# Narrowing 64-bit weights with one pass fewer, in a planned attention and MoE kernel

## The chip, the cores and the metric

One core of a Trainium2 chip runs the whole program. The metric is device time in microseconds. Three runs of the kernel before took 604.0, 604.93 and 605.22 us, a median of 604.93 us. The profiled execution took 603.86 us, of which 602.1 us lie between its first and its last instruction.

## The reference

Attention, then two gated layers, all in float32, for 4 batches of 8 heads, 512 local and 32 global positions and head size 64. The layers' weights arrive as 64-bit floats.

```python
# attention: 32 global queries see all keys; a local query sees the globals and |i-j| <= 32
out_g = sm(q_g k_all^T / 8) @ v_all
out_l = sm([q_l k_g^T / 8, where(|i-j| <= 32, q_l k_l^T / 8, -1e9)]) @ v_all
x = concat(out_g, out_l)              # (4, 544, 512) after the heads are joined

# MoE1
h = max(x @ w_in, 0)                  # 512 -> 1024
gate = sigmoid(conv over the sequence, width 3, of h)
x = (h * gate) @ w_out                # 1024 -> 512

# MoE2, with x_prev = x shifted by one position
k = max((mu_k*x + (1-mu_k)*x_prev) @ w_k, 0)
r = sigmoid((mu_r*x + (1-mu_r)*x_prev) @ w_r)
out = r * (k*k @ w_v)
```

## The kernel before

Every large product is made of three float32r matmuls: an operand is split into a rounded "hi" part and a remainder "lo", and hi*hi, hi*lo and lo*hi are added in PSUM. So each weight exists in SBUF as two tiles.

Four batches pass through attention and MoE1. Attention has a unit for each pair of heads (four units a batch): scores (`s`), masking with the row minimum on VectorE (L484), exponential on ScalarE (L491), transposes on TensorE (L500) that are copied to `eT` (L503), the product with v (L510), the division (L520 to L522), a transpose (L541) and the split into hi and lo (L548, L551). Every second unit is followed by the global queries (`glob`, L573). MoE1 of a batch (`dense`, L838) has eight blocks of H (L856, x times w_in). Each block is followed by relu (L880), three convolution taps (L889 to L898), sigmoid (L904), the product with h (L907) and the split into `gh` and `gl` (L914, L919). Then come four blocks of O (L957, times w_out), whose results are copied to a tile `xo` (L975) and stored to a DRAM tensor `x2d` (L982). There is one `xo` buffer (`XO_BUFS = 1`): the memset of its first column on GpSimd (L974) and the copies wait until the store before has landed. MoE2 (`moe2`, L1005) runs over six chunks of up to 384 tokens: K (L1094, with w_k), R (L1160, with w_r) and V (L1197, with w_v), in this order.

A 64-bit weight is narrowed to float32 (`narrow_tasks`, L701) in steps: a DMA of the raw words (SyncE's queue); the high word without its sign (L712 on ScalarE or L714 on VectorE); a maximum with the smallest normal value (`fmax`, L717, on VectorE or GpSimd); a shift left by 3 with a mask (L721, VectorE); the sign (and top bits) put back and then the low word's top bits put in (L727, two instructions, VectorE). After it come hi (L792) and lo (L795). w_in and w_out are narrowed at the start in pieces of 128x512, conv_w in one small piece. w_k, w_r and w_v are narrowed early, during the MoE1 of the batches 0 to 2, in 40 pieces of 128x256 (16, 8 and 16), which are stored to DRAM as float32 (L757). Later they are loaded again (L780) and only split: w_k and w_r when attention is done, w_v when the last H has let go of w_in's tiles, whose place it takes.

The order of instructions on each engine is written by a planner in the file (`Plan.schedule`, L198). It keeps a clock for each engine, for TensorE's speed and for each ring of buffers, takes among the tasks that could start earliest the one with the smallest key, and picks for a task with alternatives the engine that would end it first, with a bias for each engine and phase (`DVE_BIAS` and the others). The keys come from `STEP0`, `SLOT`, `LEAD`, `GAP` and the lags. VectorE and GpSimd slow each other in the plan by a factor (`PORT`, `shared`, `POOL_SLOW`). The plan only fixes the order; on the chip every instruction waits for semaphores.

Of the kernel before, what the change touches and what calls it, by code (L numbers as in the profile page):

```python
# [34 lines left out]
EST = 256  # L35
F64_MIN = float(np.array(0x38000000, np.uint32).view(np.float32))

# [4 lines left out]
ET_BUFS = 3  # L42
W2_BUFS = 6
E_STEP = 16
XB = 6
T_START = 10000
STEP0 = 6737
T_DENSE = 38000
SLOT = 72484
LEAD = 14181  # L50
GAP = 2397
GAP1 = 1480
STEPS_H = 6
E_BUFS = 4
H_FRAC = 0.5
LAG_TE = 5000
LAG_PV = 10538
LAG_G = 7061
LEAD_Q = 4000
# [4 lines left out]
LAG_TX = 9367  # L64
WINDOW = 43
FILL_MIN = 553
FILL_MARGIN = 276
FILL_START = 6
FILL_RATE = 0.478
PENALTY = 166  # L70
PHASES = (60e3, 105e3, 320e3, 375e3)
DVE_BIAS = (1550, 807, 684, 1523, 580)
ACT_BIAS = (411, 657, 466, 1004, 80)
POOL_BIAS = (6, 0, 235, 0, 113)
H_BUFS = 5
C_BUFS = 3
G_BUFS = 4
XO_BUFS = 1
V_BUFS = 3
# [3 lines left out]
QT_BUFS = 3  # L83
KT_BUFS = 4

# [61 lines left out]
class Plan:  # L147
# [16 lines left out]
    @staticmethod  # L164
    def latency(a, b):
        if a == "-" or b == "-":
            return 0
        if a == "DMA":
# [29 lines left out]
    def schedule(self):  # L198
# [13 lines left out]
        free["PE"] = 1130.0  # L212
        dve_port = False
        while cand:
            ests = []
            for t in cand:
                e = 0.0
                need = {}
                for b in t.take:
                    for r in b.rings:  # L220
                        need[r] = need.get(r, 0) + 1
                if any(len(slots[r]) < n for r, n in need.items()):
                    continue
                for r, n in need.items():
                    e = max(e, sorted(slots[r])[n - 1])
# [55 lines left out]
            if t.eng != "-":  # L281
                free[t.eng] = t.end
            if t.eng == "DVE":
                dve_port = PORT.get(t.kind, 1.0) > 1.0
            for b in t.bufs:
                owed[b] -= 1
                ends[b] = max(ends.get(b, 0.0), t.end + (1900 if t.eng == "DMA" else 200))
# [25 lines left out]
def shared(cost, left, slow):

    if left <= 0:
        return cost
    return cost * slow if left >= cost * slow else left + cost - left / slow

# [19 lines left out]
def attn_moe_kernel(  # L338
# [362 lines left out]
    def narrow_tasks(nm, load, n, braw, bmag, after, early):  # L701
# [36 lines left out]
        c = add("DVE", 68 + 534 * f, lambda: for_(1, -0x40000000, ALU.bitwise_and), deps=[c],  # L738
                use=[bmag, braw], name=f"sgn{nm}")
# [21 lines left out]

    def split_weights(nm, src, nt, ncol, pool, tag, rings, after=(), early=None):
        w = {}
# [7 lines left out]
        for k in range(nt):  # L771
            for c in range(0, ncol, WST):
                bm = buf(rings[1])
                if early:
                    t, sts = early[k, c]
                    state = {}

                    def load(t=t, c=c, bm=bm, state=state, k=k):
                        state["mag"] = alloc(bm, [P, WST], F32, f"{nm}{k}_{c}")
                        nc.sync.dma_start(out=state["mag"], in_=t[:, c : c + WST])  # L780

                    d = add("DMA", 730, load, deps=sts + [al], take=[bm], name=f"ld{nm}{k}_{c}")
                else:
                    def load(raw, k=k, c=c):
                        nc.sync.dma_start(
                            out=raw, in_=words(src[P * k : P * (k + 1), c : c + WST], "p (n t) -> p n t")
                        )

                    d, state = narrow_tasks(f"{nm}{k}_{c}", load, WST, buf(rings[0]), bm, [al], None)

                def fhi(copy, k=k, c=c, state=state):
                    copy(w["hi"][:, k, c : c + WST], state["mag"])  # L792

                def flo(e, k=k, c=c, state=state):
                    e.tensor_sub(w["lo"][:, k, c : c + WST], state["mag"], w["hi"][:, k, c : c + WST].bitcast(F32))  # L795

                h = add("ACT", 520, lambda fhi=fhi: fhi(nc.scalar.copy), deps=[d], use=[bm], name=f"hi{nm}{k}_{c}",
                        alts=[("DVE", 335, lambda fhi=fhi: fhi(nc.vector.tensor_copy))])
                l = add("POOL", 1225, lambda flo=flo: flo(nc.gpsimd), deps=[h], use=[bm], name=f"lo{nm}{k}_{c}",
                        alts=[("DVE", 602, lambda flo=flo: flo(nc.vector))])  # L800
                done[k, c] = [h, l]
        return w, done
# [35 lines left out]
    def dense(b):  # L838
# [403 lines left out]
    for b in range(B):  # L1242
# [3 lines left out]
        if b == B - 2:  # L1246
            turn_e = [0]

            def after():
# [84 lines left out]
```

## Time and profile before

| | |
|---|---|
| median of three runs | 604.93 us |
| profiled execution | 603.86 us, span 602.1 us |
| busy TensorE, VectorE, ScalarE, GpSimd | 565.3, 395.7, 285.5, 228.2 us |
| mean granted TensorE clock | 0.949 |
| DMA | 67.80 MB, nearly all through one queue |

A busy time is the union of an engine's instructions, so overlapping matmuls count once. PEclk is the granted clock as a share of the full one. In a group of instructions, the idle time "before" an instruction is what its engine stood still, and behind the arrow stands what ended it. A line number is that of the kernel before.

### The profile page before, as it was taken

How to read it: one execution, taken by the hardware profiler on the slowest of the kernel's cores; microseconds unless marked ns; L12 is line 12 of the kernel's file. 1: busy time of each engine (PE TensorE's matmuls, PEld its weight loads, DVE VectorE, ACT ScalarE, POOL GpSimd, SP SyncE). 2: the span in 40 equal slices, each digit the busy share in tenths (PEclk: the TensorE clock that was granted, in tenths of full speed). 3: DMA queues.
4: the chain of work that ended last, by engine and by line, in shares of the span. 5: the costliest groups of instructions: out<-in, count | busy, mean ns of one | idle time of the engine just before them, and what ended most of it. 6: DMA issues, size and time to landing. Idle time of an engine off the chain costs nothing. (4 is left out here: it accounts for less than half of the span.)

```text
span 602.1 us, 14503 instructions
## 1 busy us (share of the span) xinstructions
PE 565.3 (94%) x5790; PEld 515.3 (86%) x5790; DVE 395.7 (66%) x969; ACT 285.5 (47%) x632; POOL 228.2 (38%) x320
## 2 busy tenths in 40 slices
PE   8697957997999979999999899999999999999998
PEld 6585946996989879889899799889889899898897
DVE  3689999847699954999958976441826637434211
ACT  4585856614588623677466634504305225134040
POOL 3647767622243302333111554937602203203150
PEclk8787986797999979999999989999999999999999
DMA  8957701567515675005480432020110200100000
GB/s 310 339 195 246 275 10 52 179 180 233 179 54 197 193 255 174 20 3 167 170 255 16 137 126 64 8 81 18 39 67 1 62 35 1 53 19 1 36 19 35
DMA packets 34627, 67.80 MB, mean 113 GB/s; under 512 B 5120, under 2 KB 14592, under 8 KB 34560
## 3 DMA queue, kind: packets, MB, share of 16 engines
q1 hardware_dynamic: 34560, 66.88, 33.4%
q8 instruction: 45, 0.74, 0.5%
q14 instruction: 22, 0.18, 0.1%
HBM read 52.71 MB, written 14.16 MB: 111 GB/s over the span
## 5 line engine op out<-in xcount | busy, mean ns | idle before, releaser
L856 PE MATMUL ph<-x,win_hi 128*128 128x256 f32 (+1 forms) x512 | 102.4, 298 | 0.0
L957 PE MATMUL po<-gl,wout_hi 128*128 128x256 f32 (+1 forms) x256 | 77.8, 304 | 7.1 <-POOL gl L919 5.2
L957 PE MATMUL po<-gh,wout_hi 128*128 128x256 f32 (+1 forms) x256 | 79.9, 312 | 2.8 <-ACT gh L914 2.8
L856 PEld LDWEIGHTS ph<-x,win_hi 128*128 128x128 f32 x512 | 81.2, 192 | 1.4
L957 PE MATMUL po<-gh,wout_lo 128*128 128x256 f32 (+1 forms) x256 | 76.9, 300 | 0.0
L856 PE MATMUL ph<-x,win_lo 128*128 128x256 f32 (+1 forms) x256 | 74.2, 290 | 0.0
L1112 ACT ACTIVATE robuf<-pk 128x384 f32<-128x384 f32 (+1 forms) x48 | 22.7, 472 | 91.8 <-PE pk L1094 91.4
L898 DVE SCALAR_TENSOR_TENSOR c<-h,convw,c 128x544 f32<-128x544 f32 x64 | 60.2, 959 | 4.6 <-POOL h L877 2.3
L1094 PE MATMUL pk<-xkh,wkk_lo 128*128 128x384 f32 (+1 forms) x192 | 62.7, 327 | 0.0
L1094 PE MATMUL pk<-xkh,wkk_hi 128*128 128x384 f32 (+1 forms) x192 | 62.7, 327 | 0.0
L1094 PE MATMUL pk<-xkl,wkk_hi 128*128 128x384 f32 (+1 forms) x192 | 62.7, 327 | 0.0
L957 PEld LDWEIGHTS po<-gl,wout_hi 128*128 128x128 f32 x256 | 51.7, 202 | 8.0 <-POOL gl L919 5.9
L957 PEld LDWEIGHTS po<-gh,wout_hi 128*128 128x128 f32 x256 | 51.7, 202 | 4.5 <-ACT gh L914 3.2
L1197 PE MATMUL pv<-wvv_lo,k2h 128*128 128x512 f32 (+1 forms) x144 | 54.4, 378 | 0.0
L1197 PE MATMUL pv<-wvv_hi,k2h 128*128 128x512 f32 (+1 forms) x144 | 54.4, 378 | 0.0
L1197 PE MATMUL pv<-wvv_hi,k2l 128*128 128x512 f32 (+1 forms) x144 | 54.4, 377 | 0.0
L1210 DVE TENSOR_TENSOR robuf<-pv,robuf 128x512 f32<-128x512 f32 (+1 forms) x18 | 11.9, 661 | 63.5 <-PE pv L1197 63.4
L957 PEld LDWEIGHTS po<-gh,wout_lo 128*128 128x128 f32 x256 | 51.7, 202 | 0.0
L856 PEld LDWEIGHTS ph<-x,win_lo 128*128 128x128 f32 x256 | 49.0, 192 | 0.0
L491 ACT ACTIVATE e<-e 128x128 f32<-128x128 f32 x128 | 39.8, 392 | 8.8 <-DVE e L484 8.7
L1160 PE MATMUL pr<-wrr_hi,xrbuf 128*128 128x512 f32 x136 | 43.7, 395 | 0.0
L1094 PEld LDWEIGHTS pk<-xkl,wkk_hi 128*128 128x128 f32 x192 | 36.1, 188 | 0.2
(224 smaller groups left out, 1294.9 us busy)
## 6 DMA issues: line engine op xcount, KB each, us to landing
v<-in_v_l_dram SPq DMA_DIRECT2D x16, 910.0 KB, 7.1
x2d<-xo SPq DMA_DIRECT2D x16, 272.5 KB, 2.9
qT<-in_q_l_dram SPq DMA_DIRECT2D x16, 256.0 KB, 3.6
kT<-in_k_l_dram SPq DMA_DIRECT2D x16, 256.0 KB, 4.7
wout_0r<-in_moe_w_out_dram SPq DMA_DIRECT2D x8, 512.0 KB, 4.5
out_dram<-robuf SPq DMA_DIRECT2D x16, 256.0 KB, 2.0
win_0r<-in_moe_w_in_dram SPq DMA_DIRECT2D x4, 512.0 KB, 8.0
win_512r<-in_moe_w_in_dram SPq DMA_DIRECT2D x4, 512.0 KB, 7.3
```

What stands on the lines that cost most here:

```text
L491: nc.scalar.activation(be.tile[:, P * i : P * (i + 1)], be.tile[:, P * i : P * (i + 1)], AF.Exp, bias=be.tile[:, SL + i : SL + i + 1], sca ...
L856: nc.tensor.matmul(pm, lhsT=w[:, k, P * m : P * (m + 1)], rhs=x[:, s0:s1], start=(k == 0 and n == 0), stop=(k == KT - 1 and n == 2),)
L898: e.scalar_tensor_tensor(bc.tile, bh.tile[:, k : k + S], convw[:, FT * k + m : FT * k + m + 1], bc.tile, op0=ALU.mult, op1=ALU.add,)
L957: nc.tensor.matmul(pm, lhsT=w[:, k, P * m : P * (m + 1)], rhs=g[:, k % 2, s0:s1], start=(k == 0 and n == 0), stop=(k == FT - 1 and n == 2),)
L1094: nc.tensor.matmul(bp.tile[:, :n], lhsT=w[:, k, P * m : P * (m + 1)], rhs=x[:, :n], start=(k == 0 and i == 0), stop=(k == KT - 1 and i == 2),)
L1112: e.activation(kk()[:, :n], bp.tile[:, :n], AF.Relu)
L1160: nc.tensor.matmul(bp.tile, lhsT=x[:, P * j : P * (j + 1)], rhs=w[:, k], start=(k == 0 and i == 0), stop=(k == KT - 1 and i == 2),)
L1197: nc.tensor.matmul(bp.tile, lhsT=x, rhs=w[:, k, c0:c1], start=(k == 0 and i == 0), stop=(k == FT - 1 and i == 2),)
L1210: nc.vector.tensor_mul(o()[:, c0:c1], bp.tile, r()[:, c0:c1])
```

## The change

- Narrowing: the sign-free high word and the maximum are replaced by one multiplication of the high word, read as a float32, by 2^-112 on ScalarE, with no alternative on VectorE. The shift no longer masks, and the instruction that puts the sign back takes one bit.
- `w_v` is not narrowed early any more. `split_weights` narrows it from the raw words in 16 pieces of 128x256 (`EST`), with three raw buffers and three result buffers in the pool that opens after attention; as before, this can begin when the last H is done. `W2_BUFS` goes from 6 to 3.
- MoE1's output has two `xo` buffers, and its store is issued from ScalarE's queue; the planner knows that queue as an engine "AQ".
- In the planner, VectorE and GpSimd no longer slow each other by a factor. An instruction that uses the port waits until the port is free, and holds it for its whole time (VectorE kinds in `PORT`) or for 0.9 or 0.5 of it (GpSimd).
- Keys, biases, the planner's window and some ring sizes have other values (`KT_BUFS` 4 to 3).

```diff
-F64_MIN = float(np.array(0x38000000, np.uint32).view(np.float32))
+REBIAS = 2.0**-112
-W2_BUFS = 6
+W2_BUFS = 3
+W2R_BUFS = 3
-STEP0 = 6737
+STEP0 = 7159
-SLOT = 72484
-LEAD = 14181
-GAP = 2397
-GAP1 = 1480
+SLOT = 67764
+LEAD = 3854
+GAP = -8076
+GAP1 = 5974
-WINDOW = 43
+WINDOW = 25
-DVE_BIAS = (1550, 807, 684, 1523, 580)
-ACT_BIAS = (411, 657, 466, 1004, 80)
-POOL_BIAS = (6, 0, 235, 0, 113)
+DVE_BIAS = (1550, 1239, 579, 1173, -209)
+ACT_BIAS = (299, 685, -307, 215, 80)
+POOL_BIAS = (-54, 564, 227, -666, -3480)
-XO_BUFS = 1
+XO_BUFS = 2
-KT_BUFS = 4
+KT_BUFS = 3
...
-                    if o[0] == "DVE":
-                        c = shared(c, free.get("POOL", 0.0) - x, PORT.get(t.kind, 1.0))
-                    elif o[0] == "POOL":
-                        c = shared(c, free.get("DVE", 0.0) - x if dve_port else 0.0, POOL_SLOW)
+                    if holds_port(o[0], t.kind):
+                        x = max(x, free.get("PORT", 0.0))
...
+            if h := holds_port(t.eng, t.kind):
+                free["PORT"] = max(free.get("PORT", 0.0), t.start + h * t.cost)
...
+def holds_port(eng, kind):
+
+    if eng == "POOL":
+        return 0.0 if kind == "on" else 0.5 if kind in ("cv", "gn") else 0.9
+    return 1.0 if eng == "DVE" and kind in PORT else 0.0
...
-        def fabs(e):
+        def fmag():
             state["mag"] = alloc(bmag, [P, max(n, EST)], F32, f"{nm}m")[:, :n]
-            hw = state["raw"][:, :n, 1]
-            if e is nc.scalar:
-                e.activation(state["mag"], hw.bitcast(F32), AF.Abs)
-            else:
-                e.tensor_scalar(state["mag"].bitcast(I32), hw, 0x7FFFFFFF, None, op0=ALU.bitwise_and)
-
-        def fmax(e):
-            e.tensor_scalar(state["mag"], state["mag"], F64_MIN, None, op0=ALU.max)
+            nc.scalar.activation(state["mag"], state["raw"][:, :n, 1].bitcast(F32), AF.Copy, scale=REBIAS)
...
-            nc.vector.tensor_scalar(
-                bits, bits, 3, 0x3FFFFFF8, op0=ALU.logical_shift_left, op1=ALU.bitwise_and
-            )
+            nc.vector.tensor_scalar(bits, bits, 3, None, op0=ALU.logical_shift_left)
...
-        c = add("DVE", 60 + 275 * f, lambda: fmax(nc.vector), deps=[c], use=[bmag], name=f"max{nm}",
-                alts=[("POOL", 70 + 1386 * f, lambda: fmax(nc.gpsimd))])
...
-                "DMA", 900, lambda bo=bo, m=m: nc.sync.dma_start(out=x2d[b][m], in_=bo.tile),
+                "AQ", 900, lambda bo=bo, m=m: nc.scalar.dma_start(out=x2d[b][m], in_=bo.tile),
...
-                     for nm, src, nt, ncol in (("wkk", w_k, KT, FF), ("wrr", w_r, KT, DM), ("wvv", w_v, FT, DM))}
+                     for nm, src, nt, ncol in (("wkk", w_k, KT, FF), ("wrr", w_r, KT, DM))}
...
-    wvv, wvv_done = split_weights("wvv", w_v, FT, DM, lambda: winp, "wa", (None, "w2mag"), h_done + [att_done], early["wvv"])
+    wvv, wvv_done = split_weights("wvv", w_v, FT, DM, lambda: winp, "wa", ("w2raw", "w2mag"), h_done + [att_done], st=EST)
```

## Rows read from the trace of the kernel before

**Rows 1.** The page's busy times: busy us, share of the span, instructions.

```profile
PE 565.3 (94%) x5790; PEld 515.3 (86%) x5790; DVE 395.7 (66%) x969; ACT 285.5 (47%) x632; POOL 228.2 (38%) x320
```

**Rows 2.** Chain that ended last: start, length, engine, tile, line, instructions.

```profile
363.94 16.65 PE pk L1094 x96
...
388.98 16.35 PE pv L1197 x72
405.33 16.64 PE pk L1094 x96
```

**Rows 3.** Busy times by stretch, which may overlap; then clock, DMA share, GB/s.

```profile
0.00:45.00 45.00, 37.24 (x819) 31.17 (x819) 27.85 (x130) 26.63 (x73) 21.63 (x37) 0.85 0.78 282
45.00:110.00 65.00, 51.33 (x599) 45.80 (x589) 64.33 (x112) 39.99 (x84) 49.25 (x54) 0.78 0.41 140
60.00:90.00 30.00, 23.05 (x198) 22.23 (x198) 29.83 (x42) 19.68 (x41) 22.32 (x29) 0.90 0.42 146
75.00:120.00 45.00, 34.78 (x474) 31.42 (x473) 41.92 (x86) 26.06 (x57) 32.07 (x31) 0.73 0.23 79
140.00:150.00 10.00, 9.20 (x171) 8.34 (x172) 9.38 (x34) 5.72 (x15) 2.93 (x3) 0.71 0.70 221
150.00:335.00 185.00, 179.34 (x2510) 168.27 (x2509) 150.84 (x446) 117.01 (x253) 51.09 (x112) 0.98 0.43 139
335.00:389.00 54.00, 51.04 (x322) 48.80 (x321) 37.65 (x46) 25.54 (x53) 33.44 (x33) 0.97 0.28 85
```

**Rows 4.** Groups on VectorE, 60 to 90 us: count, busy us, mean ns, idle before.

```profile
L727 DVE SCALAR_TENSOR_TENSOR wout_0m<-wout_0r,wout_0m 128x512 int32<-128x512 int32 x14 | 15.0, 1081 | 0.0
L898 DVE SCALAR_TENSOR_TENSOR c<-h,convw,c 128x544 f32<-128x544 f32 x6 | 6.9, 1178 | 0.0
L721 DVE TENSOR_SCALAR wout_0m<-wout_0m 128x512 int32<-128x512 int32 x8 | 4.3, 563 | 0.0
L717 DVE TENSOR_SCALAR wout_0m<-wout_0m 128x512 f32<-128x512 f32 x4 | 4.0, 1008 | 0.0
```

**Rows 5.** Lines 727, 898, 721, 717, whole run: min/median/max ns, first and last start.

```profile
L727 DVE SCALAR_TENSOR_TENSOR wout_0m<-wout_0r,wout_0m x16: 673/750/1819, 60.1 to 94.0; 128x512 int32<-128x512 int32 x16
...
L898 DVE SCALAR_TENSOR_TENSOR c<-h,convw,c x64: 765/778/1859, 65.5 to 339.8; 128x544 f32<-128x544 f32 x64
...
L721 DVE TENSOR_SCALAR wout_0m<-wout_0m x8: 412/415/1395, 59.5 to 89.6; 128x512 int32<-128x512 int32 x8
...
L717 POOL TENSOR_SCALAR wout_0m<-wout_0m x4: 1503/1838/1908, 56.8 to 71.2; 128x512 f32<-128x512 f32 x4
L717 DVE TENSOR_SCALAR wout_0m<-wout_0m x4: 414/1001/1618, 62.5 to 86.3; 128x512 f32<-128x512 f32 x4
```

**Rows 6.** Timeline of VectorE and GpSimd, 337 to 340 us: start, length.

```profile
337.33 0.78 DVE L898 SCALAR_TENSOR_TENSOR c<-h,convw,c 128x544 f32<-128x544 f32 x1
337.56 1.74 POOL L919 TENSOR_TENSOR gl<-c,gh 128x544 fp32r<-128x544 f32 x1 [4.88 <-DVE gh L914]
338.02 1.86 DVE L907 TENSOR_TENSOR c<-c,h 128x544 f32<-128x544 f32 x1
```

**Rows 7.** Timeline, 139 to 141 us: start, length, engine; idle before, releaser.

```profile
139.58 0.68 ACT L975 COPY xo<-po 128x256 f32<-128x256 f32 x2 [2.98 <-DMA x2d<-xo]
...
140.14 1.10 ACT L503 COPY eT<-pe 128x512 f32<-128x512 f32 x2
...
140.80 0.45 PE L510 MATMUL o<-v,eT 128*32 128x65 f32 x8 [3.67 <-ACT eT L503]
```

**Rows 8.** Waits by pair: us in total, times, longest.

```profile
ACT xo L975 <- DMA x2d<-xo: 14.7, 7, 4.5
```

**Rows 9.** Lines 727 and 721 on w_v's first half pieces, min/median/max ns.

```profile
L727 DVE SCALAR_TENSOR_TENSOR ewvv_0m<-ewvv_0r,ewvv_0m x16: 406/418/640, 221.0 to 298.5; 128x256 int32<-128x256 int32 x16
...
L721 DVE TENSOR_SCALAR ewvv_0m<-ewvv_0m x8: 279/282/433, 220.7 to 297.5; 128x256 int32<-128x256 int32 x8
```

**Rows 10.** DMA issues: KB each, median us to landing.

```profile
ewvv_256r<-in_moe_w_v_dram SPq DMA_DIRECT2D x8, 256.0 KB, 4.0
```

More of the change, by code (lines that the diff above doesn't have):

```diff
@@ L46 @@
 T_START = 10000
-STEP0 = 6737
+STEP0 = 7159
 T_DENSE = 38000
-SLOT = 72484
-LEAD = 14181
-GAP = 2397
-GAP1 = 1480
+SLOT = 67764
+LEAD = 3854
+GAP = -8076
+GAP1 = 5974
 STEPS_H = 6
 E_BUFS = 4
[L55 to L58, printed above, removed]
+H_FRAC = 0.498
+LAG_TE = 3810
+LAG_PV = 10382
+LAG_G = 5305
 LEAD_Q = 4000
@@ L69 @@
 FILL_RATE = 0.478
-PENALTY = 166
+PENALTY = 394
 PHASES = (60e3, 105e3, 320e3, 375e3)
-DVE_BIAS = (1550, 807, 684, 1523, 580)
-ACT_BIAS = (411, 657, 466, 1004, 80)
-POOL_BIAS = (6, 0, 235, 0, 113)
+DVE_BIAS = (1550, 1239, 579, 1173, -209)
+ACT_BIAS = (299, 685, -307, 215, 80)
+POOL_BIAS = (-54, 564, 227, -666, -3480)
 H_BUFS = 5
@@ L167, in latency @@
             return 0
-        if a == "DMA":
+        if a in ("DMA", "AQ"):
             return 1900
@@ L212, in schedule @@
         free["PE"] = 1130.0
-        dve_port = False
         while cand:
@@ L282, in schedule @@
                 free[t.eng] = t.end
-            if t.eng == "DVE":
-                dve_port = PORT.get(t.kind, 1.0) > 1.0
+            if h := holds_port(t.eng, t.kind):
+                free["PORT"] = max(free.get("PORT", 0.0), t.start + h * t.cost)
             for b in t.bufs:
                 owed[b] -= 1
-                ends[b] = max(ends.get(b, 0.0), t.end + (1900 if t.eng == "DMA" else 200))
+                ends[b] = max(ends.get(b, 0.0), t.end + (1900 if t.eng in ("DMA", "AQ") else 200))
                 if not owed[b]:
@@ L304 @@
 WEIGHTS = ("win", "wout", "wkk", "wrr", "wvv", "conv")
-POOL_SLOW = 1.17
 PORT = {
-    "cv": 1.55, "mu": 1.65, "gl": 1.65, "gh": 3.0, "max": 1.6, "shl": 1.6, "sgn": 1.15, "low": 1.15, "lo": 1.65,
-    "hi": 3.0, "d": 1.65, "xxk": 1.9, "xxr": 1.9, "xkh": 3.0, "xrh": 3.0, "xkl": 1.65, "xrl": 1.65, "sq": 1.65,
-    "k2h": 3.0, "k2l": 1.65, "gn": 2.0,
-}
[L313 to L317, printed above, removed]
+    "cv", "mu", "gl", "gh", "max", "shl", "sgn", "low", "lo", "hi", "d", "xxk", "xxr", "xkh", "xrh", "xkl", "xrl", "sq",
+    "k2h", "k2l", "gn",
+}
+def holds_port(eng, kind):
+    if eng == "POOL":
+        return 0.0 if kind == "on" else 0.5 if kind in ("cv", "gn") else 0.9
+    return 1.0 if eng == "DVE" and kind in PORT else 0.0
 def bias(eng, x):
@@ L351, in attn_moe_kernel @@
         "x0": XB, "x1": XB, "h": H_BUFS, "c": C_BUFS, "gh": G_BUFS, "gl": G_BUFS, "xo": XO_BUFS,
-        "w2mag": W2_BUFS,
+        "w2mag": W2_BUFS, "w2raw": W2R_BUFS,
     })
@@ L732, in narrow_tasks @@
         a = add("DMA", 1460 * f, fload, deps=after, take=[braw], name=f"ld{nm}")
-        c = add("ACT", 40 + 480 * f, lambda: fabs(nc.scalar), deps=[a], take=[bmag], use=[braw], name=f"abs{nm}",
-                alts=[("DVE", 60 + 275 * f, lambda: fabs(nc.vector))])
-        c = add("DVE", 60 + 275 * f, lambda: fmax(nc.vector), deps=[c], use=[bmag], name=f"max{nm}",
-                alts=[("POOL", 70 + 1386 * f, lambda: fmax(nc.gpsimd))])
+        c = add("ACT", 90 + 490 * f, fmag, deps=[a], take=[bmag], use=[braw], name=f"abs{nm}")
         c = add("DVE", 60 + 275 * f, fshift, deps=[c], use=[bmag], name=f"shl{nm}")
-        c = add("DVE", 68 + 534 * f, lambda: for_(1, -0x40000000, ALU.bitwise_and), deps=[c],
+        c = add("DVE", 68 + 534 * f, lambda: for_(1, -0x80000000, ALU.bitwise_and), deps=[c],
                 use=[bmag, braw], name=f"sgn{nm}")
@@ L760, in early_narrow, with split_weights @@
         return pieces
-    def split_weights(nm, src, nt, ncol, pool, tag, rings, after=(), early=None):
+    def split_weights(nm, src, nt, ncol, pool, tag, rings, after=(), early=None, st=WST):
         w = {}
@@ L771, in split_weights @@
         for k in range(nt):
-            for c in range(0, ncol, WST):
+            for c in range(0, ncol, st):
                 bm = buf(rings[1])
@@ L785, in load @@
                         nc.sync.dma_start(
-                            out=raw, in_=words(src[P * k : P * (k + 1), c : c + WST], "p (n t) -> p n t")
+                            out=raw, in_=words(src[P * k : P * (k + 1), c : c + st], "p (n t) -> p n t")
                         )
-                    d, state = narrow_tasks(f"{nm}{k}_{c}", load, WST, buf(rings[0]), bm, [al], None)
+                    d, state = narrow_tasks(f"{nm}{k}_{c}", load, st, buf(rings[0]), bm, [al], None)
                 def fhi(copy, k=k, c=c, state=state):
-                    copy(w["hi"][:, k, c : c + WST], state["mag"])
+                    copy(w["hi"][:, k, c : c + st], state["mag"])
                 def flo(e, k=k, c=c, state=state):
[L795 to L801, printed above, removed]
+                    e.tensor_sub(w["lo"][:, k, c : c + st], state["mag"], w["hi"][:, k, c : c + st].bitcast(F32))
+                f = st / WST
+                h = add("ACT", 40 + 480 * f, lambda fhi=fhi: fhi(nc.scalar.copy), deps=[d], use=[bm], name=f"hi{nm}{k}_{c}",
+                        alts=[("DVE", 60 + 275 * f, lambda fhi=fhi: fhi(nc.vector.tensor_copy))])
+                l = add("POOL", 70 + 1155 * f, lambda flo=flo: flo(nc.gpsimd), deps=[h], use=[bm], name=f"lo{nm}{k}_{c}",
+                        alts=[("DVE", 68 + 534 * f, lambda flo=flo: flo(nc.vector))])
+                done.setdefault((k, c // WST * WST), []).extend([h, l])
         return w, done
@@ L1261, in open_w2 @@
                 w2["p"] = ctx.enter_context(tc.tile_pool(name="w2", bufs=1, side="right"))
-                pools["w2mag"] = w2["p"]
+                pools["w2mag"] = pools["w2raw"] = w2["p"]
             att_done = add("-", 0, open_w2, deps=att_tasks, name="open_w2")
```

## The prediction

> **What bounds the kernel now.** I read the busy times first, then the chain that ended last, then the busy times by stretch. TensorE is busy 565.3 of 602.1 us [rows 1]. From 363.94 us on the chain is TensorE alone, K, R and V chunk after chunk without a gap: 16.65 us of K, then R, and V from 388.98 us [rows 2]. That is 238 us of the span that no other engine can shorten, as long as its operands are there. The reader should therefore look for the time ahead of 364 us, in two forms: TensorE idle, and TensorE at a low clock.
>
> The stretches show where [rows 3]. In them a clock of 1 is TensorE's upper level of 2.4 GHz and 0.5 its lower one of 1.2 GHz; a mean between is a stretch that had both. From 150 to 335 us TensorE is busy 179.3 of 185 us at a clock of 0.98, so little is left there. From 45 to 110 us it is VectorE that is full, 64.33 of 65 us, while TensorE has 51.33 us at a clock of 0.78. That is the stage in which w_out is narrowed beside the first batch's MoE1. Between 140 and 150 us the clock is 0.71 again. The price of the early stage is paid in VectorE time, and the later dips are single waits.
>
> **VectorE and GpSimd share something, and the stage pays for it.** A GpSimd instruction of 1.74 us starts at 337.56 us. A VectorE product with both inputs in SBUF, issued at 338.02 us, takes 1.86 us and ends just after it [rows 6], and the shortest times of such forms are far below: 673 ns for L727 and 765 ns for L898, with 1819 and 1859 ns at the other end [rows 5]. For 60 to 90 us I add up what VectorE lost to this, mean less shortest, by count [rows 4, 5]: L727 14 x (1081 - 673) = 5.7 us, L898 6 x (1178 - 765) = 2.5, L721 8 x (563 - 412) = 1.2, L717 4 x (1008 - 414) = 2.4, together 11.8 us. GpSimd was busy 22.32 us in it [rows 3]. So by this estimate a microsecond of GpSimd costs VectorE about 11.8 / 22.32 = 0.53 us there.
>
> **The change part by part**, against the profiled execution's 603.86 us, which lies 1.07 us under the median.
>
> *The maximum goes.* For w_out four of the eight maxima were on VectorE, 4.0 us in all [rows 4]. The other four were on GpSimd, at a median of 1838 ns [rows 5], 7.4 us, which at 0.53 gives VectorE 3.9 us back. VectorE has no gap in this stage, so I take all of it as an earlier end: 7.9 us. The upper end is that GpSimd blocks VectorE for its whole length, 4.0 + 7.4 = 11.4 us. The lower end is 0, if another engine then holds TensorE in that stage. The maxima of w_in lie mostly before 45 us, where VectorE has 27.85 of 45 us [rows 3], and I give them nothing. What is late next is the chain of ScalarE passes and GpSimd's lo parts.
>
> The Trainium skill ("SBUF — State Buffer", section "Who interferes with whom") says that the port pair of VectorE and GpSimd is locked for a whole instruction and the loser waits, not shares. The stretched product above agrees with it; the 0.53 does not contradict it, since GpSimd is not always in VectorE's way. By the rule alone the term would be the 11.4 us of the upper end, and the sum 3.5 us lower.
>
> *The first pass has ScalarE alone.* Its multiplication takes the place of the pass without a sign, and the few such passes that VectorE did go to ScalarE too. ScalarE has 25 of 65 us free in the full stage [rows 3], so I put this at nothing. If that cover were gone, a pass over a piece would cost about as much as one of the two `eT` copies of the same 512 columns that took 1.10 us together [rows 7], and for two passes it would be 1.1 us.
>
> *Two buffers for the output, stored from ScalarE's queue.* With one buffer ScalarE waited 14.7 us for landed stores, at most 4.5 us at a time [rows 8]. Most of that stands beside full matmuls. One wait does not: at 139.58 us ScalarE comes out of a wait of 2.98 us, only then copies `eT`, and TensorE has stood 3.67 us for it [rows 7]. Behind it TensorE works at 0.71 from 140 to 150 us [rows 3], which costs (1 - 0.71) x 10 = 2.9 us. With a second buffer the copy needs the store before last, so I take both back, 6.6 us. The lower end is 0 (the copy could be late for another reason), and on the wrong side stands up to 4.5 us, the longest wait of ScalarE [rows 8]: the store now stands in ScalarE's own order and waits for both copies, one of which may be VectorE's, and sigmoid, relu and the `eT` copies queue behind it. SyncE's queue loses these waits, so loads behind them start earlier; I price that at nothing, since those loads are for buffers that are needed later.
>
> *w_v narrowed late.* Its 16 pieces leave the stretch from 150 to 335 us, where VectorE had 34 us free and TensorE was full, so nothing is won there. They land between the last H, at about 335 us, and the first V at 388.98 us [rows 2]. VectorE needs for a piece one L721 and two L727, 282 + 2 x 418 = 1118 ns [rows 9], so 17.9 us for 16; the hi and lo passes were there before. VectorE has 54 - 37.65 = 16.4 us free in that stretch [rows 3]. It lacks 1.5 us, and a first piece has to be loaded, so I take a delay of 2 us for the first V. Loading does not decide: 4.0 us for a load [rows 10] and some 1.7 us of passes, in three buffers, is 16 x 5.7 / 3 = 30 us of the 54. The good end is 0, because preparations for the second chunk can go behind the first V (K of that chunk starts at 405.33 us [rows 2]). The bad end is a rival below.
>
> *The planner's order and the values.* The order of every engine is new. A bound on each side comes from the rows: what the full stage still has in TensorE idle after the terms above, 65 - 51.33 - 7.9 = 5.8 us, could go; or one wait of the kind just described, 3.67 + 2.9 us, could appear elsewhere. I take 0. `KT_BUFS` at 3 and the narrower window go with it.
>
> Sum: 603.86 - 7.9 - 6.6 + 2 = 591.4 us, and with the 1.07 us between the profiled execution and the median, 592.4 us.
>
> **Rivals.**
>
> A, better: with VectorE relieved the matmuls of 75 to 120 us come without gaps and the clock stays up. TensorE was busy 34.78 us there at 0.73 [rows 3]; at the full clock that is 25.4 us, 9.4 us less, so 583.0 us. For it: the low clock follows the gaps in that stage. Against: VectorE is still nearly full after 7.9 of 64.33 us are gone.
>
> B, the relief of the first stage is hidden: the second batch's attention, which ScalarE and the loads also hold, starts H no earlier, and of the sum only the wait of 3.67 us goes. That is 604.93 - 3.7 = 601.2 us. For it: ScalarE and GpSimd are also well used in 45 to 110 us, 39.99 and 49.25 us [rows 3]. Against: both have more room than VectorE.
>
> C, slower: the first V waits for w_v. VectorE's work for w_v is of the kind that GpSimd stretches, and GpSimd is busy 33.44 of the 54 us [rows 3]. At the ratio of the stage of w_out, 1081 / 673 = 1.61, its 17.9 us become 28.8, 12.4 us more than are free. TensorE then stands for 12.4 us, and the first V of 16.35 us [rows 2] runs at a clock like the 0.73 after the gaps of the first stage, 16.35 / 0.73 - 16.35 = 6 us more: 18.4 us in place of the 2, so 608.8 us. It decides from a wait of about 14.5 us on, which is what the first two terms give. For it: the narrowing cannot start before 335 us. Against: preparations for later chunks can give way.
>
> **How the numbers follow.** The forecast (585 to 599 us) has 0.46, A and beyond (below 585) 0.18, B (599 to 603.7) 0.12, a time within 0.2% of 604.93 us, which is about what a measurement can tell from no change, 0.06, and C or another slower order 0.18. So faster has 0.46 + 0.18 + 0.12 = 0.76. For 8 times in 10 the range reaches below A to 578 us and up to C at 609 us; I leave some 0.1 out on each side, because the order as a whole is new.
>
> **What would show it.** Right: no L717 row; the mean of L727 on w_out nearer to 673 ns than 1081; VectorE leaving its full stage before 105 us; no wait of ScalarE's L975 for a landed store ahead of `eT`; the chain's TensorE part starting near 350 us. The w_v term is right if TensorE stands at most some 2 us before the first V. Wrong: the first V waits for wvv_lo by many microseconds, ScalarE stands before its own DMA issues, or TensorE gets new gaps between 150 and 335 us at a lower clock than 0.98.

## The result

The changed kernel takes 584.47 us (median of 4 runs, 580.32 to 591.67) beside 605.08 us for the kernel before: a ratio of 0.9635, 95% interval 0.9575 to 0.9696, so 20.6 us less by the medians (22 by the ratio) where 12.5 were forecast. A repeat, e9 below, gave 0.968 (0.9628 to 0.9732). The time lies inside the range of 578 to 609 us, but just below the forecast's own 585 to 599: it falls to "A and beyond", which had a chance of 0.18, 1.5 us from rival A's 583.0. Ratios leave disturbed runs out (591.67 is one), medians don't, and e8's profiled execution is the only disturbed one that is quoted.

The profiled execution took 585.69 us. The chain of waits, as start, length, engine, tile, line and instructions, answers to [rows 2]:

```profile
350.30 12.06 PE pk L1079 x68
362.36 8.39 PE pr L1145 x36
370.75 16.35 PE pv L1182 x72
```

The first V starts at 370.75 us and not at 388.98, 18.2 us earlier, which is also what the profiled executions differ by (603.86 - 585.69). From there on both kernels run the same TensorE chain. Everything was gained before the first V. The two chains enter K at different places: 363.94 us was K's start (x96), 350.30 us is within K (x68). K itself starts at 343.5 us, some 20 us earlier than before. The page's busy times, to be held against [rows 1]:

```profile
PE 559.5 (96%) x5792; PEld 510.3 (87%) x5792; DVE 354.6 (61%) x926; ACT 273.9 (47%) x619; POOL 208.4 (36%) x331
```

The stretches of [rows 3], with three more; columns as there:

```profile
0.00:45.00 45.00, 39.39 (x723) 33.03 (x723) 25.11 (x127) 24.47 (x64) 10.18 (x32) 0.77 0.82 288
45.00:110.00 65.00, 58.91 (x1136) 53.13 (x1137) 60.85 (x176) 54.44 (x127) 32.73 (x47) 0.95 0.52 180
60.00:90.00 30.00, 28.16 (x408) 26.91 (x410) 28.30 (x61) 24.19 (x51) 16.26 (x30) 0.96 0.39 141
75.00:120.00 45.00, 40.85 (x895) 35.46 (x893) 41.95 (x140) 39.01 (x88) 23.29 (x26) 0.96 0.47 160
110.00:140.00 30.00, 30.00 (x395) 28.52 (x394) 20.61 (x80) 17.25 (x46) 5.18 (x11) 1.00 0.68 210
140.00:190.00 50.00, 45.30 (x519) 43.21 (x523) 38.34 (x83) 31.66 (x66) 4.42 (x24) 0.90 0.44 141
150.00:335.00 185.00, 176.60 (x2184) 166.47 (x2183) 129.31 (x329) 118.64 (x254) 16.51 (x75) 0.96 0.32 102
190.00:335.00 145.00, 141.29 (x1763) 133.26 (x1752) 95.63 (x260) 90.72 (x197) 12.35 (x55) 0.99 0.31 98
335.00:389.00 54.00, 52.73 (x284) 47.44 (x284) 42.44 (x75) 26.34 (x64) 33.81 (x38) 1.00 0.32 101
```

The same view of the kernel before, for the three stretches that [rows 3] lacks:

```profile
110.00:140.00 30.00, 27.13 (x312) 25.77 (x310) 15.56 (x65) 11.07 (x32) 10.77 (x18) 0.96 0.66 213
140.00:190.00 50.00, 48.23 (x843) 44.25 (x844) 42.89 (x146) 37.37 (x81) 18.09 (x34) 0.94 0.43 133
190.00:335.00 145.00, 140.31 (x1835) 132.36 (x1835) 117.33 (x334) 85.35 (x188) 35.93 (x81) 0.98 0.44 147
```

TensorE's busy time times its granted clock is an estimate of its work in microseconds at the full clock (the clock is the mean of the whole stretch, its idle time too). From 45 to 110 us it went from 51.33 x 0.78 = 40.0 to 58.91 x 0.95 = 56.0; from 110 to 140 us from 26.0 to 30.0; from 140 to 190 us from 45.3 down to 40.8; from 190 to 335 us from 137.5 to 139.9; in the first 45 us from 31.7 to 30.3. Together 16.5 us more by 335 us, nearly all of it from 45 to 140 us.

What that work was shows in two views. First, the matmuls of O (w_out), 192 a batch, by stretch: TensorE's busy time with them, weight loads, clock, DMA share, GB/s. Of the kernel before, with stretches cut where each batch's O ends:

```profile
0.00:135.50 135.50, 29.77 (x192) 28.46 (x192) 0.84 0.57 199
135.50:233.50 98.00, 29.04 (x192) 26.58 (x192) 0.93 0.58 188
233.50:311.50 78.00, 27.18 (x192) 24.73 (x192) 1.00 0.36 119
311.50:364.50 53.00, 26.61 (x192) 25.92 (x192) 0.97 0.33 102
```

And of the changed kernel, cut in the same way:

```profile
0.00:139.50 139.50, 24.84 (x192) 24.18 (x192) 0.90 0.65 221
139.50:217.50 78.00, 27.63 (x192) 24.80 (x192) 0.93 0.48 158
217.50:290.50 73.00, 27.30 (x192) 24.71 (x192) 1.00 0.15 50
290.50:345.00 54.50, 26.34 (x192) 25.85 (x192) 0.97 0.44 131
```

The first batch ends 4 us later than before (139.3 and 135.1 us), but in e9's execution of the same kernel at 134.0 us, so it ends about as before. The second takes 78 us after it and not 98, the third 73 and not 78, the fourth 54 and not 53.5; e9 has the same three lengths within 1 us. Second, one of the two groups of score matmuls (64 to an attention unit) of the kernel before, in the full stage and after it:

```profile
45.00:110.00 65.00, 2.85 (x128) 2.16 (x128) 0.78 0.41 140
145.00:330.00 185.00, 7.97 (x512) 6.25 (x512) 0.98 0.43 142
```

and of the changed kernel:

```profile
45.00:110.00 65.00, 5.51 (x320) 4.31 (x320) 0.95 0.52 180
145.00:330.00 185.00, 4.98 (x320) 3.90 (x320) 0.96 0.32 103
```

Five units where there were two: attention of the next batches now fills the gaps of the first batch's MoE1, and batches 1 and 2 have less left to do. The relief of VectorE wasn't spent on ending the stage earlier but on giving TensorE other work in it.

VectorE in the stage itself, 60 to 90 us (count, busy us, mean ns, idle before), answers to [rows 4]:

```profile
L714 DVE SCALAR_TENSOR_TENSOR wout_0m<-wout_0r,wout_0m 128x512 int32<-128x512 int32 x14 | 11.3, 838 | 0.0
L883 DVE SCALAR_TENSOR_TENSOR c<-h,convw,c 128x544 f32<-128x544 f32 x6 | 6.4, 1069 | 0.7 <-POOL c L880 0.7
L710 DVE TENSOR_SCALAR wout_0m<-wout_0m 128x512 int32<-128x512 int32 x6 | 4.0, 672 | 0.7 <-ACT wout_0m L706 0.7
```

L714 is the old L727, L883 the old L898, L710 the old L721. With the shortest times of [rows 5] VectorE lost 14 x (838 - 673) = 2.3 us, 6 x (1069 - 765) = 1.8 us and 6 x (672 - 412) = 1.6 us to GpSimd, 5.7 us in all where before it was 11.8. Over the whole run 14 of the 16 L714 on w_out take 673 to 687 ns, and 13 of these have no GpSimd instruction beside them; the other two, beside a GpSimd subtraction, take 1793 and 1779.

The waits of the changed kernel (us in total, times, longest) that bear on the store and on the new gaps:

```profile
POOL xo L959 <- DMA x2d<-xo: 26.8, 4, 9.0
ACT xo L960 <- PE po L942: 13.3, 14, 2.4
PE o L506 <- ACT eT L499: 3.9, 2, 3.5
```

ScalarE's wait for a landed store [rows 8] has no successor. But TensorE has a gap of 3.5 us for `eT` again, now ahead of 160 us, with a clock of 0.51 from 160 to 170 us behind it, and 140 to 190 us is the one long stretch that got worse. Behind the last O TensorE stands twice, 0.78 and 0.49 us, both within K. The first:

```profile
348.82 0.45 PE L1079 MATMUL pk<-xkl,wkk_hi 128*128 128x384 f32 x1 [0.78 <-DVE xkl L1042]
```

### The profile page after: what moved, and what is told of

The parts are those of the page before. It is cut to its first block, busy times and chain, and to the rows that moved or that the text cites. A ratio compares the mean times of both kernels' runs of the same rounds, so it can differ in the third digit from the quotient of the medians.

```text
span 583.9 us, 14463 instructions
## 1 busy us (share of the span) xinstructions
PE 559.5 (96%) x5792; PEld 510.3 (87%) x5792; DVE 354.6 (61%) x926; ACT 273.9 (47%) x619; POOL 208.4 (36%) x331
## 5 line engine op out<-in xcount | busy, mean ns | idle before, releaser
L942 PE MATMUL po<-gh,wout_hi 128*128 128x288 f32 (+1 forms) x256 | 77.2, 301 | 2.4 <-ACT gh L899 2.4
L942 PE MATMUL po<-gl,wout_hi 128*128 128x288 f32 (+1 forms) x256 | 74.6, 291 | 1.3 <-DVE gl L904 1.3
L841 PE MATMUL ph<-x,win_lo 128*128 128x288 f32 (+1 forms) x256 | 74.2, 290 | 0.0
L942 PE MATMUL po<-gh,wout_lo 128*128 128x288 f32 (+1 forms) x256 | 74.1, 290 | 0.0
L1109 ACT CAST k2h<-robuf 128x384 fp32r<-128x384 f32 (+1 forms) x29 | 14.3, 498 | 100.8 <-POOL robuf L1102 100.6
L883 DVE SCALAR_TENSOR_TENSOR c<-h,convw,c 128x544 f32<-128x544 f32 x64 | 51.1, 808 | 10.2 <-ACT c L876 7.6
L1102 POOL TENSOR_TENSOR robuf<-robuf 128x384 f32<-128x384 f32 (+1 forms) x45 | 36.8, 822 | 51.1 <-DVE robuf L1099 47.5
L942 PEld LDWEIGHTS po<-gh,wout_hi 128*128 128x128 f32 x256 | 48.9, 191 | 3.7 <-ACT gh L899 2.6
L942 PEld LDWEIGHTS po<-gl,wout_hi 128*128 128x128 f32 x256 | 48.9, 191 | 1.5 <-DVE gl L904 1.5
L1114 POOL TENSOR_TENSOR k2l<-robuf,k2h 128x384 fp32r<-128x384 f32 (+1 forms) x46 | 45.3, 1001 | 7.1 <-DVE k2h L1109 5.4
L487 ACT ACTIVATE e<-e 128x128 f32<-128x128 f32 x128 | 40.1, 393 | 9.0 <-DVE e L480 9.0
```

The lines of the kernel that those rows point to most:

```text
L487: nc.scalar.activation(be.tile[:, P * i : P * (i + 1)], be.tile[:, P * i : P * (i + 1)], AF.Exp, bias=be.tile[:, SL + i : SL + i + 1], sca ...
L841: nc.tensor.matmul(pm, lhsT=w[:, k, P * m : P * (m + 1)], rhs=x[:, s0:s1], start=(k == 0 and n == 0), stop=(k == KT - 1 and n == 2),)
L883: e.scalar_tensor_tensor(bc.tile, bh.tile[:, k : k + S], convw[:, FT * k + m : FT * k + m + 1], bc.tile, op0=ALU.mult, op1=ALU.add,)
L942: nc.tensor.matmul(pm, lhsT=w[:, k, P * m : P * (m + 1)], rhs=g[:, k % 2, s0:s1], start=(k == 0 and n == 0), stop=(k == FT - 1 and n == 2),)
L1102: e.tensor_mul(ks()[:, :n], kk()[:, :n], kk()[:, :n])
L1109: copy(bg[0].tile[:, m % 2, :n], ks()[:, :n])
```

## The experiments

Ratios are to the kernel before, timed on the same chip. Theory: a better first stage, made of the missing maximum, of the order and of what each lets the other do. Rivals: the second `xo` buffer; late w_v; the order alone.

**e1: the maximum gone, the old order kept.** The planner still books its time, but it emits nothing.

```diff
-                e.activation(state["mag"], hw.bitcast(F32), AF.Abs)
+                e.activation(state["mag"], hw.bitcast(F32), AF.Copy, scale=REBIAS)
...
-            e.tensor_scalar(state["mag"], state["mag"], F64_MIN, None, op0=ALU.max)
+            pass
```

> The kernel before, planned as before and so in its own order on every engine, but the maximum emits nothing and the first pass multiplies by 2^-112 on the engine it had. Theory 1 (the maximum's VectorE time in the full stage ends it earlier, as the prediction has it): 7.9 us less, about 597 us, with VectorE's L727 on w_out nearer 673 than 1081 ns. Theory 2 (the gain is in the new order, and an order made for the maximum cannot use the freed time): within 3 us of the kernel before, 602 to 606 us.

596.98 us, 0.988 (0.9829 to 0.9932): 7.65 us less, against a term of 7.9. K starts at 353.70 us, 10.2 us earlier in the profile. The full stage of e1:

```profile
45.00:110.00 65.00, 53.12 (x645) 48.03 (x645) 62.25 (x120) 43.17 (x93) 40.77 (x48) 0.82 0.42 143
```

TensorE's work there is 53.12 x 0.82 = 43.6 us, up 3.6. VectorE is nearly as full as before, 62.25 of 65 us: the gain came through, but the stage was not opened up. O of batch 0 ends 4.1 us earlier, at 131.0; the rest comes in later batches. The time met the expectation, its sign did not: the mean of L727 on w_out (below) is 1142 ns and not nearer 673.

**e2: two `xo` buffers, stored from ScalarE's queue, old order.** The `eT` ring goes from 3 to 2 to make room. **e0: that smaller ring alone**, as the control.

```diff
-        b.tile = pool.tile(shape, dtype, tag=b.tag, name=name, bufs=plan.rings[b.tag])
+        b.tile = pool.tile(shape, dtype, tag=b.tag, name=name, bufs={"eT": 2, "xo": 2}.get(b.tag, plan.rings[b.tag]))
...
-                "DMA", 900, lambda bo=bo, m=m: nc.sync.dma_start(out=x2d[b][m], in_=bo.tile),
+                "DMA", 900, lambda bo=bo, m=m: nc.scalar.dma_start(out=x2d[b][m], in_=bo.tile),
```

> The kernel before in its own order, with two xo buffers and the store issued from ScalarE's queue; the place is paid by a ring of two eT buffers in place of three. Theory 1 (the wait of ScalarE for a landed store held TensorE 3.67 us at 139 us and lowered its clock behind that): 3.7 to 6.6 us less, 598 to 601 us, no wait of L975 for the DMA x2d. Theory 2: the wait goes and another takes its place at once, 604 to 606 us; the smaller eT ring can even cost a few us.

> The kernel before in its own order with two eT buffers in place of three and nothing else: the control for e2_xo2_act, which came out 3.4 us slower than the kernel before. If the smaller eT ring is what cost it, 610 us or more (then two xo buffers are worth some us); if the eT ring costs nothing, 604 to 606 us, and the two xo buffers with ScalarE's store are worth nothing or less in this order.

e2: 608.02 us, 1.0068 (1.0041 to 1.0095), 3 to 4 us slower than the kernel before. e0: 604.78 us, 1.0033 (0.9991 to 1.0076), so the ring by itself costs nothing that can be told. Against this control e2 is 2 us slower by the ratios, with intervals that overlap. In e2 ScalarE's wait for the store is gone, and other waits stand instead:

```profile
ACT xo L975 <- PE po L957: 16.3, 9, 3.3
PE X L541 <- DVE xn L522: 9.1, 6, 4.2
```

The 14.7 us that ScalarE waited were not in TensorE's way, or TensorE then waited for the next late thing. The term of 6.6 us is refuted in the old order.

**e4: the new order, the old content.** The port rule, keys, biases and `KT_BUFS` of the change, with the maximum, one `xo` buffer, SyncE's store and early w_v.

```diff
-SLOT = 72484
-LEAD = 14181
+SLOT = 67764
+LEAD = 3854
...
-                    if o[0] == "DVE":
-                        c = shared(c, free.get("POOL", 0.0) - x, PORT.get(t.kind, 1.0))
+                    if holds_port(o[0], t.kind):
+                        x = max(x, free.get("PORT", 0.0))
```

> The content of the kernel before (maximum, one xo buffer, SyncE's store, w_v narrowed early) planned with the new port rule and the new keys, biases and KT_BUFS 3. The prediction's term for this was 0: 603 to 607 us. Theory 2 (the order is the gain): 588 to 595 us, with TensorE's clock between 75 and 120 us at 0.9 or more.

598.03 us, 0.9891 (0.9828 to 0.9955): 6.6 us less with no instruction saved. That lies between the two expected ranges, and the clock from 75 to 120 us is 0.86 and not 0.9. Its full stage:

```profile
45.00:110.00 65.00, 53.50 (x825) 47.76 (x818) 56.18 (x153) 43.05 (x97) 40.09 (x47) 0.89 0.48 164
```

The work there is 47.6 us, more than e1 reached by doing less. The narrowing instruction on w_out shows a part of it. In the kernel before its 16 instructions have a mean of 1098 ns; in e1, over the first 150 us (count, busy us, mean ns, idle):

```profile
L727 DVE SCALAR_TENSOR_TENSOR wout_0m<-wout_0r,wout_0m 128x512 int32<-128x512 int32 x16 | 18.0, 1142 | 0.1
```

and in e4, in the same view:

```profile
L722 DVE SCALAR_TENSOR_TENSOR wout_0m<-wout_0r,wout_0m 128x512 int32<-128x512 int32 x16 | 10.1, 681 | 0.0
```

It is the order, not the missing maximum, that spares these 16 instructions. But in e4 it doesn't keep the two engines apart: nine of the 16 have a GpSimd product beside them, and run at full speed all the same. The one that is stretched is GpSimd's (timeline, start, length):

```profile
72.36 4.29 DVE L722 SCALAR_TENSOR_TENSOR wout_0m<-wout_0r,wout_0m 128x512 int32<-128x512 int32 x7
72.51 6.38 POOL L902 TENSOR_TENSOR c<-c,h 128x544 f32<-128x544 f32 x1 [1.76 <-DVE c L893]
```

GpSimd's six products of this kind in e4 have a median of 1.48 us. Here VectorE started first and went on without a break, and GpSimd stood beside it. So GpSimd's 40.09 us in this stage, close to e1's 40.77, are in part such standing.

**e7: the new content, the old order's rule and keys.** **e12: the new content and keys, with only the old slowing factors in place of the port rule**, planned anew.

```diff
-                    if holds_port(o[0], t.kind):
-                        x = max(x, free.get("PORT", 0.0))
+                    if o[0] == "DVE":
+                        c = shared(c, free.get("POOL", 0.0) - x, PORT.get(t.kind, 1.0))
+                    elif o[0] == "POOL":
+                        c = shared(c, free.get("DVE", 0.0) - x if dve_port else 0.0, POOL_SLOW)
```

(e7 has the old `SLOT`, `LEAD`, lags and biases beside it.)

> The content of the changed kernel (no maximum, two xo buffers and ScalarE's store, w_v narrowed late, KT_BUFS 3) planned with the old slowing factors, keys and biases. Theory 1 (content is the gain, as in the prediction's sum): 590 to 595 us. Theory 2 (the order is the gain): 600 us or more.

> The changed kernel planned anew with its keys and biases, but with the old slowing factors between VectorE and GpSimd in place of the exclusive port. If the port rule is what made the order good: 592 us or more. If the keys and biases alone did: 583 to 588 us. (The keys go with the rule, so a loss here does not show how the rule does with other keys.)

e7: 612.69 us, 1.0125 (1.008 to 1.017). e12: 611.87 us, 1.0118 (1.0073 to 1.0162). Both are slower than the kernel before, with the maximum gone. Two stretches of e12, the full stage and the one from 335 us:

```profile
45.00:110.00 65.00, 50.79 (x595) 46.43 (x591) 60.53 (x116) 41.52 (x87) 38.47 (x48) 0.79 0.37 128
...
335.00:389.00 54.00, 42.11 (x267) 39.88 (x266) 48.53 (x76) 26.71 (x64) 34.27 (x36) 0.91 0.42 124
```

and of e7:

```profile
45.00:110.00 65.00, 53.89 (x646) 48.36 (x642) 57.50 (x122) 41.46 (x83) 38.34 (x45) 0.82 0.36 125
...
335.00:389.00 54.00, 42.87 (x257) 41.35 (x257) 46.79 (x76) 26.25 (x64) 33.29 (x36) 0.84 0.42 124
```

In e12 the first stage is back at 50.79 x 0.79 = 40.1 us of work, the value of the kernel before. In both TensorE stands for over 11 of the 54 us ahead of the first V, where w_v is narrowed. The timeline of e7 in its first K (start, length, engine; idle before, releaser):

```profile
367.65 0.41 ACT L781 CAST wvv_hi<-wvv_0m 128x256 fp32r<-128x256 f32 x1 [1.34 <-DVE wvv_0m L719]
...
370.36 0.62 DVE L1033 SCALAR_TENSOR_TENSOR xt0xk<-d,mus,x 128x384 f32<-128x384 f32 x1 [0.89 <-POOL xo L964]
...
370.77 0.51 ACT L1043 CAST xkh<-xt0xk 128x384 fp32r<-128x384 f32 x1 [0.98 <-POOL xo L964]
...
371.33 0.69 PE L1084 MATMUL pk<-xkh,wkk_hi 128*128 128x384 f32 x1 [4.44 <-ACT xkh L1043]
```

K has stood 4.44 us for `xkh`, one of its own operands. ScalarE makes it after a pass of w_v that waited for VectorE's narrowing, and VectorE makes its source late, behind w_v's passes and the last `xo`. The first V starts at 397.49 us. This is rival C's crowding, at K, one step ahead of where the prediction put it.

**e8: a pass of the maximum's kind put back on VectorE, in the changed kernel.** Planned as before; a maximum with -3e38, which changes nothing in the data.

```diff
         def fshift():
+            nc.vector.tensor_scalar(state["mag"], state["mag"], -HUGE, None, op0=ALU.max)
```

> The changed kernel in its own order, with a maximum (against a huge negative number, so nothing is altered) put back on VectorE before each shift. Theory 1 (VectorE's time in the first stage is worth its length in the new order too; 16 passes of 128x512 at 0.41 us are 6.6 us, and 24 of 128x256 at 0.28 us more of 6.7 us lie under full matmuls): 590 to 593 us. Rival (the new order has slack on VectorE there, 60.85 of 65 us): 584 to 588 us.

598.47 us, 0.988 (0.9827 to 0.9934): by the ratios 12 to 15 us more than the changed kernel, for 17 instructions and 9.1 us of VectorE in the first 110 us, 24 under the later batches (7.1 us) and 16 in w_v's narrowing (5.4 us). Both expected ranges were too low. Its full stage, and the O matmuls (busy us, weight loads, clock, DMA share, GB/s) that still ran when the changed kernel had finished batch 0:

```profile
45.00:110.00 65.00, 55.66 (x905) 49.96 (x904) 57.81 (x158) 44.92 (x107) 27.10 (x41) 0.84 0.49 169
...
139.50:151.50 12.00, 11.09 (x89) 10.86 (x87) 1.00 0.58 177
```

Batch 0 ends about 11 us later, and the work from 45 to 110 us is 46.8 and not 56.0 us. Of the 17.3 us between the two profiled executions (602.97 and 585.69) 12.3 are there when the last O ends; the other 5.0 come between it and the first V, where the 16 passes stand in w_v's narrowing. So the 12 to 15 us are not the price of the first stage's 9.1 us alone, and whether a pass there is worth more than its length isn't shown.

**e5: w_v narrowed early again, in the changed kernel**, planned anew.

```diff
-W2_BUFS = 3
+W2_BUFS = 6
...
-    wvv, wvv_done = split_weights("wvv", w_v, FT, DM, lambda: winp, "wa", ("w2raw", "w2mag"), h_done + [att_done], st=EST)
+    wvv, wvv_done = split_weights("wvv", w_v, FT, DM, lambda: winp, "wa", (None, "w2mag"), h_done + [att_done], early["wvv"])
```

> The changed kernel planned anew with w_v narrowed early to DRAM as before (six w2mag buffers of 128x512). Theory 1 (late w_v costs 2 us before the first V, and its leaving the MoE1 stages gives nothing because TensorE is full there): 582 to 585 us. Rival (its 40 VectorE and ScalarE passes and its DMAs in the third batch's stage delay attention): 588 us or more, with the O of batch 2 ending later than 290 us.

588.93 us, 0.9783 (0.9697 to 0.9869): 4 us more than the changed kernel by the medians, 6 to 9 by the ratios, with an interval that begins where the first timing's ends and overlaps e9's. O of batch 2 ends at 296.2 us, against 289.7, as the rival had it. The stretch from 150 to 335 us:

```profile
150.00:335.00 185.00, 171.76 (x2133) 161.03 (x2132) 139.05 (x364) 121.27 (x260) 15.74 (x73) 0.96 0.42 133
```

VectorE has 9.7 us more there than in the changed kernel and TensorE 4.8 us less. In exchange the first V follows without a wait:

```profile
351.86 16.65 PE pk L1079 x96
...
376.91 16.35 PE pv L1182 x72
```

**e9: the changed kernel again, e10 and e6: with one `xo` buffer, e11: with two, stored from SyncE.** e6 and e10 are the same kernel, e10 timed in more rounds beside e9.

```diff
-        b.tile = pool.tile(shape, dtype, tag=b.tag, name=name, bufs=plan.rings[b.tag])
+        b.tile = pool.tile(shape, dtype, tag=b.tag, name=name, bufs=1 if b.tag == "xo" else plan.rings[b.tag])
```

and for e11

```diff
-                "AQ", 900, lambda bo=bo, m=m: nc.scalar.dma_start(out=x2d[b][m], in_=bo.tile),
+                "AQ", 900, lambda bo=bo, m=m: nc.sync.dma_start(out=x2d[b][m], in_=bo.tile),
```

> The changed kernel in its own order, with one xo buffer. If two buffers are worth what the prediction gave them, 6.6 us: 590 us or more, with waits of ScalarE or GpSimd for the DMA x2d in front of eT copies. If they are worth nothing: 583 to 587 us.

> The changed kernel once more, as the base for the three beside it on the same chip: 583 to 586 us.

> e6_xo1 once more (the changed kernel in its own order with one xo buffer), beside its base, since its first interval overlapped that of the changed kernel. Two buffers worth about 5 us: 588 to 590 us. Worth nothing: 583 to 586 us, within 2 us of the base.

> The changed kernel in its own order, two xo buffers, but the store issued from SyncE's queue as before. If the queue itself is worth something (SyncE's loads no longer wait behind copies of xo): 587 us or more. If not: within 2 us of the base.

e6: 589.1 us, 0.9776 (0.962 to 0.9932), too wide to tell. e9: 584.84 us, 0.968 (0.9628 to 0.9732). e10: 586.76 us and e11: 586.91 us, both 0.971 (0.9663 to 0.9756). The differences of 1.9 and 2.1 us from e9 lie inside the intervals. In e10 the waits for the store are back,

```profile
POOL xo L959 <- DMA x2d<-xo: 89.5, 11, 22.7
...
ACT xo L960 <- DMA x2d<-xo: 15.0, 5, 3.7
```

as long as in the kernel before on ScalarE, and they cost next to nothing. The two buffers and the queue are worth some 2 us at most by the medians; which of them, or whether either, stays open.

The full stage against the time, sorted by the first (busy time times clock, 45 to 110 us):

| kernel | work, us | time, us |
|---|---|---|
| before | 40.0 | 605.1 |
| e12 old slowing factors | 40.1 | 611.9 |
| e0 smaller `eT` ring | 41.3 | 604.8 |
| e2 two `xo`, old order | 41.5 | 608.0 |
| e1 no maximum, old order | 43.6 | 597.0 |
| e7 new content, old rule and keys | 44.2 | 612.7 |
| e8 a pass put back | 46.8 | 598.5 |
| e4 new order, old content | 47.6 | 598.0 |
| e11 store from SyncE | 51.2 | 586.9 |
| e5 early w_v | 52.2 | 588.9 |
| e6 one `xo` | 52.4 | 589.1 |
| e10 one `xo` | 55.8 | 586.8 |
| changed kernel | 56.0 | 584.5 |
| e9 changed kernel again | 56.7 | 584.8 |

Work and time go roughly together except in e7 and e12, where the first V starts 9.7 and 11.6 us later behind the last O than K and R take (25.05 us). The work is of one execution, the time a median: e6 and e10 are the same kernel and lie 3.4 us apart.

## Why the prediction came out as it did

Direction and range held; the forecast was 8 us too careful, and the time fell just outside its own 585 to 599. The first mis-sized term is **"The planner's order and the values ... I take 0"**, with 6 us as its bound on either side. Alone it measured -6.6 us (e4). With the new content it decides the sign: the content that is 20.6 us faster in the new order is 7 to 8 us slower than before under the old factors (e7, e12), a difference of 27 us. The prediction treated the order as noise around a sum of parts. The maximum has its value in the old order too (e1); late w_v has not: under the old factors it comes with 9.7 and 11.6 us of delay behind the last O, 2 to 4 in the new order. (The new content without late w_v under the old factors wasn't run, so its share of the 27 us isn't known.) Caution: keys and biases belong to the port rule, and e12 changes the rule alone with keys chosen beside it, so the rule's own share isn't separated.

The sum came as near as it did by luck: -6.6 us that the buffers did not give stood where the order gave -6.6. And the single parts add up: 0.988 (e1) x 0.9891 (e4) = 0.977, and the changed kernel with early w_v (e5) measured 0.9783. What is left to 0.9635 and 0.968, some 6 to 9 us, goes with late w_v, as far as e5's wide interval tells.

- *The maximum, -7.9.* Right in size in the old order, -7.65 (e1); in the new order a pass put back costs 12 to 15 us (e8), but that includes 16 passes behind the last O, which the term of -7.9 doesn't cover. The mechanism was half right: VectorE's time was the bound, but "an earlier end" was only about half of it. In e1 the first batch ends 4.1 us earlier and L727's mean rose to 1142 ns, so that 7.65 meets 7.9 is in part luck. In the changed kernel it ends at 139.3 us, in e9's execution at 134.0, where it was 135.1.
- *First pass on ScalarE alone, 0.* Right: the multiplication has a median of 670 ns on a w_out piece, the pass without a sign had 669 ns, and ScalarE still has 10.6 us free from 45 to 110 us.
- *Two buffers and the queue, -6.6.* Refuted. The wait named did go, as forecast, and TensorE waits for `eT` 3.5 us elsewhere. Worth +2 to +4 in the old order (e2 against e0, and against the kernel before) and not told from 0 in the new (e10, e11). The wrong-side bound of 4.5 us was the better guide. The step that failed is "so I take both back": one stall of 3.67 us that a wait caused was taken as gone, when the next late operand stood right behind it.
- *Late w_v, +2.* The size of the wait is right, its place is not: O ends at 343.7 us, K and R take 25.05, the first V starts at 370.75, 2.0 us late, but V follows R without a gap. It is K that stands, 0.78 and then 0.49 us, for its operand `xkl`, which VectorE makes among w_v's passes (shown above). In e9's execution the gaps are 1.16 and 0.49 us, the clock dips behind them (0.94 from the last O to the first V), and V is 4.2 us late. "So nothing is won there" most likely failed: early narrowing takes 9.7 us of VectorE from 150 to 335 us and the kernel was 4 to 9 us slower (e5, whose interval overlaps e9's), although VectorE had room there by its sum.
- *Rivals.* A came closest: the clock from 75 to 120 us went from 0.73 to 0.96 as it said. But its price rested on unchanged work at a better clock, where in fact TensorE had 895 matmuls there and not 474. C's mechanism exists (e7, e12), at the first K, and the order decides how far it goes. B is refuted by e1.
- *What would show it.* No maximum and no store wait ahead of `eT`: yes. The chain near 350 us: yes by the letter, 350.30, but by chance, since that is within K, which starts at 343.5. The mean of L727 on w_out nearer 673 than 1081: yes, 838 ns in 60 to 90 us, but due to the order (e1 1142, e4 681), not to the missing maximum. VectorE out of its full stage before 105 us: no, 41.95 of 45 us from 75 to 120. New gaps between 150 and 335 us, the sign against it: they came (176.60 of 185 us at 0.96), and cost less than the early stage gave.

Open: what a pass in the first stage alone costs in the new order (e8 puts passes behind the last O too); how much late w_v gives and how much of the 27 us it takes under the old factors; whether the second `xo` buffer and ScalarE's queue are worth 0 or 2 us; the port rule without its keys. No version that was run beats the changed kernel.

## What to carry to other kernels

Where an order is planned, price a change of content together with the order it is planned in: test the content in the old order and the order with the old content before you add terms. Look at the bounding stage for work per microsecond (busy time times clock) as well as for its end, because freed time may be filled with the next batch's work. A long wait of an engine off the chain, even one with a TensorE gap behind it, is worth only the distance to the next late operand.

## What the runs showed of the hardware

**The order decides which of VectorE and GpSimd is stretched, and a run of instructions can keep the other standing for all of it.** With the port rule in e4 the 16 narrowing instructions on w_out lie between 673 and 687 ns; before they reached 1819 ns [rows 5]. The forms, counts and engine are the same:

```profile
L722 DVE SCALAR_TENSOR_TENSOR wout_0m<-wout_0r,wout_0m x16: 673/681/687, 61.4 to 110.4; 128x512 int32<-128x512 int32 x16
```

The Trainium skill ("SBUF — State Buffer", section "Who interferes with whom") says that whoever issues first has the shared ports for the whole instruction and the loser waits. The traces agree with it: in e1 VectorE lost, with a mean of 1142 ns, and in e4 GpSimd lost, 6.38 us for a product beside seven of these instructions (shown above) where the median is 1.48.

**Two executions of the same program differ from the first stage on.** e9's profiled execution took 582.22 us and the one above 585.69. The first 45 us of e9:

```profile
0.00:45.00 45.00, 37.28 (x904) 32.01 (x905) 28.91 (x140) 28.70 (x77) 11.54 (x32) 0.92 0.82 300
```

At 37.28 x 0.92 = 34.3 us of work against 39.39 x 0.77 = 30.3, there is a lead of 4 us from the start. O of batch 0 ends 5.3 us earlier in e9 (134.0), the last O 5.7 (338.0); K gives 2.2 us of it back, and 3.5 us are left. What set off the lower clock in the first 45 us isn't shown. Runs of the changed kernel spread from 580 to 592 us, those of the kernel before from 604.0 to 606.5 beside them and from 598.4 to 607.9 beside e9; a difference of 2 us can't be told in that.
